# Handing the last 672 columns of the mixer's output weights to nine of the 16 DMA engines

## The chip, the cores and the metric

One core of one Trainium2 chip runs the kernel. The time is the device time of one execution in microseconds, taken as a median of several executions. Differences below 0.3 us matter, so small differences are read from the traces as well as from the times.

## The reference, cut to what matters

A decode step. An attention block (32 query heads, 4 key/value heads, 65,536 cached keys of 128 values) and a small gated mixer work on one row of 1,024 values, and a sigmoid gate mixes their two results.

```python
g = _sigmoid((x * gate_w).sum(-1, keepdims=True))
a = _A_ref(x, A_k_cache, A_v_cache, A_wq, A_wo)     # attention over the caches
b = _B_ref(x, B_w_in, B_w_sp, B_b_sp, B_w_out)      # mixer: B_w_out is 1792 x 1024
return g * a + (1 - g) * b
```

The caches and the weights are 162 MB, each byte read once. For a single row of queries there is little arithmetic, so the work is to stream those bytes (before the change the loads fill 98.9% of the span of 16 DMA engines).

## The kernel before

All large loads go through one queue, in a fixed order, into slots of a ring in SBUF. A load of 128 rows is one instruction on the sync engine (SP):

```python
def load(keys, src, off):
    n = len(stream)
    w = src.shape[1]
    ...
    stream.append((keys, off, src))

load([("wq", 0)], rows(A_wq, 0, 8), VB)
load_k2(0, 0)
load([("win", 0)], rows(B_w_in, 0, 8), VB)
load_k(2, 2)
load_k(3, 0)
load([("wout", 0)], rows(B_w_out, 0, 14), VB)      # 128 rows of 14 x 1024 columns, 28,672 bytes each
...                                                # caches, then the attention's output weights
# in issue():
P("SP", lambda e, o=OFF["RING"] + off, w=w, src=src: e.dma_start(arena[:, o:o + w], src),
  w=[("slot", x) for x in gr], dma="s%d" % gr[0])
```

The last six loads are the attention's output weights. Matmuls on them, one copy and a store of 2 KB end the program.

## Time and profile before

| | before |
|---|---|
| median time, us | 381.85 (381.81 to 382.06, 6 runs) |
| span of the profiled run, us | 380.3 |
| share of 16 DMA engines' span that the loads fill | 98.9% |
| landings of the last load, first and last engine, us | 376.57 and 378.23 |
| mean landing of the last load over 16 engines, us | 377.49 |

A landing is the moment at which one DMA engine reports that its share of a load has arrived, by an increment of the load's semaphore; the last load, of 128 rows, has 16 of them in the trace, as has every other load of 128 rows. PE is the matmul engine, DVE the vector engine. The main lines of the page stand in the prediction below. Two more views of the kernel before matter later. The first is the sync engine's queue in order of time (start us, us, engine and line, operation, out<-in, count): the load that the change cuts is issued at 65.81, and nothing more is issued until 79.62.

```profile
65.81 0.33 SPq L389 DMA_DIRECT2D arena<-in_B_w_out_dram  x1
79.62 0.33 SPq L389 DMA_DIRECT2D arena<-in_A_k_cache_dram  x1
```

The second is the DMA view of 84.5 to 87.3 us, the time in which the last rows of that load run (queue and kind: packets, MB, share of 16 engines):

```profile
q1 hardware_dynamic: 37, 1.19, 100.1%
```

A packet counts in the window in which it starts, with its whole duration, so a share can pass 100%. What is to be read is the ratio of the last two numbers: here 1.19 MB took 100.1% of 16 x 2.8 us, which is 37.7 us of engine time for a MB. This is the price of undisturbed streaming.

### The profile page before, as it was taken

To read this page: it belongs to the slowest core of one execution; us is meant where nothing else is said; L and a number is where in the kernel's file an instruction comes from. 1 tells how busy PE (TensorE), PEld (TensorE's weight loads), DVE (VectorE), ACT (ScalarE), POOL (GpSimd) and SP (SyncE) were. 2 spreads that over 40 slices of the span, in tenths; PEclk is the share of its full clock that TensorE was granted. 3 is DMA by queue.
4 is the path that set the end of the run, shared out by engine and by line. 5 is a ranking of instruction groups with operands and counts; after the bars stand their busy time and mean duration, and the time that the engine had idled before them with its cause. 6 is when DMAs were issued, how large, how long until landed. Compare 5 with 4: busy or idle time off the path is not lost.

```text
span 380.3 us, 2581 instructions
## 1 busy us (share of the span) xinstructions
PE 235.1 (62%) x1449; PEld 58.1 (15%) x836; DVE 204.6 (54%) x162; ACT 23.3 (6%) x24; POOL 8.4 (2%) x37
## 2 busy tenths in 40 slices
PE   0061388458558924895788138952895884739378
PEld 0010011011111200122112001220121110212015
DVE  4011496778389525965892249745774882312020
ACT  1000000010420000002200000022000000220000
POOL 5000000000000000000000000000000000000000
PEclk9998599696859985998699859995899697958689
DMA  9999999999999999999999999999999999999996
GB/s 435 427 420 400 469 388 438 441 469 431 401 414 441 441 443 427 434 410 424 477 441 434 434 434 414 415 441 441 434 407 433 445 441 441 436 403 424 419 426 262
DMA packets 4254, 162.17 MB, mean 426 GB/s; under 512 B 532, under 2 KB 532, under 8 KB 788
## 3 DMA queue, kind: packets, MB, share of 16 engines
q1 hardware_dynamic: 4208, 162.01, 98.9%
q8 instruction: 9, 0.15, 0.2%
q10 hardware_dynamic: 36, 0.00, 0.0%
q14 instruction: 1, 0.01, 0.0%
HBM read 162.01 MB, written 0.00 MB: 426 GB/s over the span
## 4 chain that ended last, share of the span: by engine, by line
DMA 56%; PE 23%; DVE 18%; ACT 1%; issue 1%; SPq 0%; ACTq 0%; DVEq 0%
DMA arena<-in_A_k_cache_dram 34%; DVE arena L502 15%; DMA arena<-in_A_wo_dram 10%; DMA arena<-in_A_v_cache_dram 8%; PE scp L260 7%; PE scp L262 6%; DMA arena<-in_B_b_sp_dram 5%; PE obt L260 4%; PE obt L262 4%; DVE arena L539 1%; PE fbt L712 1%; PE fbt L660 1%; ACT arena L534 1%; SPq L389 0%; ACTq L288 0%
## 5 line engine op out<-in xcount | busy, mean ns | idle before, releaser
L502 DVE STREAM_TRANSPOSE arena<-arena 128x2048 f32<-128x2048 f32 x64 | 143.0, 2284 | 48.2 <-DMA arena<-in_A_k_cache_dram 32.7
L260 PE MATMUL scp<-arena 128*128 128x512 bf16 (+1 forms) x275 | 112.8, 429 | 87.7 <-DVE arena L502 86.3
L262 PE MATMUL scp<-arena 128*128 128x512 bf16 (+1 forms) x279 | 113.1, 427 | 0.0
L260 PE MATMUL obt<-arena 128*64 128x512 bf16 (+2 forms) x334 | 62.9, 419 | 17.5 <-DMA arena<-in_A_v_cache_dram 17.5
L262 PE MATMUL obt<-arena 128*64 128x512 bf16 (+2 forms) x334 | 62.2, 414 | 0.0
L260 PEld LDWEIGHTS scp<-arena 128*128 128x128 bf16 (+1 forms) x275 | 27.7, 104 | 200.1 <-issue 101.3
L539 DVE STREAM_TRANSPOSE arena<-arena 128x2048 bf16<-128x2048 bf16 x7 | 16.2, 2311 | 28.5 <-PE obt L262 26.4
L534 ACT ACTIVATE arena<-arena 128x2048 bf16<-128x2048 f32 x8 | 16.0, 2002 | 218.6 <-DVE arena L531 195.6
L260 PEld LDWEIGHTS obt<-arena 128*64 128x64 bf16 (+1 forms) x334 | 18.3, 113 | 70.7 <-issue 56.1
L519 DVE TENSOR_SCALAR_CACHE_REDUCE arena<-scp 128x2048 f32<-128x2048 f32 x8 | 18.3, 2292 | 16.0 <-PE scp L262 16.0
L580 PE MATMUL mbt<-arena 128*128 128x128 bf16 x16 | 1.9, 258 | 12.6 <-DVE arena L575 12.6
L542 DVE STREAM_TRANSPOSE arena<-arena 128x1024 bf16<-128x1024 bf16 x2 | 2.5, 1246 | 12.7 <-PE obt L262 12.7
L490 POOL COPY arena<-arena 32x32 bf16<-32x32 bf16 x16 | 3.2, 203 | 234.5 <-PE scp L262 209.7
L568 DVE RECIPROCAL arena<-mbt 128x1 f32<-128x1 f32 x4 | 0.6, 139 | 14.1 <-PE mbt L563 14.1
L531 DVE TENSOR_REDUCE arena<-mbt 128x1 f32<-128x32 f32 x4 | 0.8, 192 | 13.5 <-PE mbt L528 13.5
L437 PE MATMUL mbt<-arena 1*128 1x2 bf16 x1 | 0.2, 158 | 12.3 <-DMA arena<-in_B_b_sp_dram 12.3
L439 DVE COPY arena<-mbt 128x2 f32<-128x2 f32 x1 | 0.2, 160 | 12.3 <-PE mbt L437 12.3
L775 DVE CAST arena<-fbt 36x128 bf16<-36x128 f32 x1 | 0.3, 283 | 11.0 <-PE fbt L712 11.0
L432 PE MATMUL scp<-arena 8*128 8x1 bf16 x8 | 0.7, 199 | 8.7 <-DVE arena L427 8.7
L712 PE MATMUL fbt<-arena 128*32 128x128 bf16 x128 | 4.1, 220 | 0.1
L712 PEld LDWEIGHTS fbt<-arena 128*32 128x32 bf16 x128 | 3.6, 97 | 1.6 <-DMA arena<-in_A_wo_dram 0.8
L467 DVE CAST arena<-obt 97x1024 bf16<-97x1024 f32 x1 | 1.2, 1225 | 4.9 <-PE obt L262 4.9
(91 smaller groups left out, 54.2 us busy)
## 6 DMA issues: line engine op xcount, KB each, us to landing
arena<-in_A_k_cache_dram SPq DMA_DIRECT2D x6, 4096.0 KB, 33.1
arena<-in_A_v_cache_dram SPq DMA_DIRECT2D x2, 4096.0 KB, 26.0
arena<-in_B_w_in_dram SPq DMA_DIRECT2D x1, 7168.0 KB, 30.4
arena<-in_A_wo_dram SPq DMA_DIRECT2D x3, 2048.0 KB, 33.4
arena<-in_B_w_out_dram SPq DMA_DIRECT2D x1, 3584.0 KB, 21.5
arena<-in_A_wo_dram SPq DMA_DIRECT2D x1, 1280.0 KB, 30.3
arena<-in_A_wo_dram SPq DMA_DIRECT2D x1, 512.0 KB, 31.0
arena<-in_A_wo_dram SPq DMA_DIRECT2D x1, 256.0 KB, 30.8
```

The source lines that it names most:

```text
L260: return e.matmul(*a, **kw)
L262: one = e.matmul(*a, **kw).ins
L467: P("DVE", lambda e: e.tensor_copy(psb[0:97, :], ob[0:97, :]), w=["psb", "ob"])
L490: P("POOL", lambda e, pb=pb: e.tensor_copy(vw(qpad, 24 + 32 * pb, [[QP, 4], [1, 8]], 32 * pb, 32), vw(qall, 8 * g, [[32, 4], [1, 8]], 32 * ...
L502: P("DVE", lambda e: e.transpose(ktb(i).bitcast(F32), sl[:, 4096 * p:4096 * (p + 1)].bitcast(F32)), r=keys[4 * p:4 * p + 4], w=[("kt", i % ...
L519: P("DVE", lambda e: e.tensor_scalar(scs(j), scp[:, :], 0.0, None, op0=ALU.add, op1=ALU.max, accum_out=maxc[:, j:j + 1]), w=[("sc", j % 2) ...
L534: P("ACT", lambda e: e.activation(psb2, scs(j), ACTF.Exp, bias=gcol(j // 2, K_NB), scale=SCALE, accum_out=lp[:, j:j + 1]), r=[("sc", j % 2 ...
L539: P("DVE", lambda e: e.transpose(ptsb2, psb2), r=["psb"], w=[("ptsb", 0), ("ptsb", 1)])
L542: P("DVE", lambda e: e.transpose(ptsb(n), ab("PSB", 1024, 1024 * (n % 2))), r=["psb"], w=[("ptsb", n % 2)])
L580: ins = e.matmul(mb[:, 0:128], sel[:, 128 * c:128 * (c + 1)], osc[:, 128 * c:128 * (c + 1)], start=(c == 0), stop=(c == 3))
L660: ins = e.matmul(fb[32 * b:32 * (b + 1), 0:QW], e4z[0:97, 31 - j:63 - j], part[0:97, QW * s:QW * (s + 1)], start=(first and s % (NW // 2) ...
L712: ins = e.matmul(fb[32 * b:32 * (b + 1), 0:QW], ovz[:, z:z + 32], sl[:, o:o + QW], start=False, stop=(i == 3 and c == 7), tile_position=(0 ...
```

## The change

Its intent is to even out when the 16 DMA engines finish. The last 672 of the 14,336 columns are cut off and loaded as three further loads of 69, 54 and 5 rows, so that some engines carry more and the others less.

```diff
-    def load(keys, src, off):
+    def load(keys, src, off, cut=None):
...
+        dst = arena[:, OFF["RING"] + off:OFF["RING"] + off + w]
+        parts = [(dst, src)]
+        if cut:
+            c, heights = cut
+            parts = [(dst[:, 0:w - c], src[:, 0:w - c])]
+            p = 0
+            for h in heights:
+                parts.append((dst[p:p + h, w - c:w], src[p:p + h, w - c:w]))
+                p += h
+            assert p == 128
+        stream.append((keys, off, w, parts))
...
-    load([("wout", 0)], rows(B_w_out, 0, 14), VB)
+    load([("wout", 0)], rows(B_w_out, 0, 14), VB, cut=(672, (69, 54, 5)))
...
-            P("SP", lambda e, o=OFF["RING"] + off, w=w, src=src: e.dma_start(arena[:, o:o + w], src),
-              w=[("slot", x) for x in gr], dma="s%d" % gr[0])
+            P("SP", lambda e, todo=todo: [e.dma_start(dst, x) for dst, x in todo],
+              w=[("slot", x) for x in gr], dma="s%d" % gr[0], parts=len(todo))
```

The rest of the diff lets one recorded operation issue several loads and count all their completions on one semaphore.

More of the change, by code (lines that the diff above doesn't have):

```diff
@@ L29, in __init__, with op @@
         self.early = 0
-    def op(self, eng, fn, r=(), w=(), dma=None):
+    def op(self, eng, fn, r=(), w=(), dma=None, parts=1):
         o = Op()
@@ L50, in op @@
         if dma is not None:
-            self.dma_count[dma] = self.dma_count.get(dma, 0) + 16
+            self.dma_count[dma] = self.dma_count.get(dma, 0) + 16 * parts
             o.dma = (dma, self.dma_count[dma])
@@ L112, in run @@
                 if o.dma:
-                    last.then_inc(dsem[o.dma[0]], 16)
+                    for x in last if isinstance(last, list) else [last]:
+                        x.then_inc(dsem[o.dma[0]], 16)
                 elif o.inc:
@@ L312, in load @@
             place[key] = (n, off + i * (w // len(keys)), w // len(keys))
-        stream.append((keys, off, src))
+        dst = arena[:, OFF["RING"] + off:OFF["RING"] + off + w]
[9 more added lines that the diff above has]
+        stream.append((keys, off, w, parts))
     def rows(w, i, c):
@@ L379, in issue @@
             n = issued[0]
-            keys, off, src = stream[n]
-            w = src.shape[1]
+            keys, off, w, todo = stream[n]
             gr = grains(off, w)
```

## The prediction

- The numbers of engines are names. 0 to 7 are the eight chains that carry the first store's packets (eight landings, 376.11 to 377.59 us: four early, one middle, three late). That the three engines of the 69 rows, 0 to 2, lie among these eight was the assumption.
- That 69, 54 and 5 rows run on 3, 9 and 5 engines was not in the trace of before. The trace after the change bears it out: 33 packets of 4 bytes where 16 stood (the 480 of the program before are 16 for each of 29 loads of 128 rows and 8 for each of two stores of 8 rows), which is 16 + 3 + 9 + 5, and short rows on nine chains of 16, so that the loads of 69 and of 5 rows run on engines of the load of 54. The 23 + 6 + 1 = 30 rows on each of three engines are an estimate from these counts.
- "Ports" is the name of the first rival. It says that engines 9 to 15, "those", slow down by what they were spared.

The last engine's end goes from 1.79 to 1.46 us behind the first, 0.33 us, and 381.96 - 0.33 = 381.63 was put at 381.7.

> **What bounds the kernel now.** I read the page first: the DMA row of the 40 slices, the queue table, the chain that ended last. Then the chain in order of time for the last 14 us, and last the trace's records of single DMA packets and of semaphore landings. Three parts of the page:
>
> ```profile
> span 380.3 us, 2581 instructions
> ...
> DMA  9999999999999999999999999999999999999996
> ...
> q1 hardware_dynamic: 4208, 162.01, 98.9%
> q8 instruction: 9, 0.15, 0.2%
> ...
> DMA 56%; PE 23%; DVE 18%; ACT 1%; issue 1%; SPq 0%; ACTq 0%; DVEq 0%
> ```
>
> The reader is to see that the 16 DMA engines never rest: the queue of loads (q1) fills 98.9% of 16 engines' span, and PE (62%) and DVE (54%) have room. 162 MB over 380 us is 426 GB/s, so only bytes, or an uneven share of them, can move the end. Small beside q1 stand nine instruction packets (q8); I use them below. The tail of the chain in order of time (start us, us, what):
>
> ```profile
> 331.05 37.33 DMA arena<-in_A_wo_dram
> 368.38 0.04 issue
> 368.42 0.39 PE scp L260 x4
> ...
> 376.41 0.08 issue
> 376.50 1.77 PE fbt L712 x56
> 378.27 0.01 issue
> 378.27 0.42 PE fbt L712 x8
> 378.69 0.03 issue
> 378.72 0.02 DVEq L110
> 378.74 0.04 issue
> 378.79 0.28 DVE arena L775
> ```
>
> The reader is to see that PE starts at 368.42 on the landing of an output-weight block and has no real pause afterwards; the last 8 matmuls start at 378.27, when the last load has just landed (378.23). So the end follows the last loads one to one. And the DMA share in windows over the last microseconds (window; us, PE, PEld, DVE, ACT, POOL, PEclk, DMA share, GB/s):
>
> ```profile
> 375.00:376.00 1.00, 1.00 (x26) 0.58 (x19) 0.00 (x0) 0.00 (x0) 0.00 (x0) 1.00 0.98 393
> 376.00:377.00 1.00, 0.92 (x21) 0.54 (x21) 0.00 (x0) 0.00 (x0) 0.00 (x0) 1.00 0.65 257
> 377.00:378.00 1.00, 1.00 (x43) 0.97 (x38) 0.00 (x0) 0.00 (x0) 0.00 (x0) 1.00 0.41 150
> ```
>
> The share falls from 0.98 to 0.65 to 0.41 ahead of the last landing: some engines have run out of work while others still carry the last rows. That is the only slack the change can use.
>
> **How uneven it is.** The 16 increments of the last load's semaphore land at 376.57, .57, .60, .61, .65, then 376.96 and 377.07, then nine from 377.89 to 378.23. So five engines end 1.6 us before the last, two 1.2 to 1.3 us, nine within 0.35 us of it. The first load shows a spread of only 0.51 us (21.435 to 21.949). The lateness is collected on the way: each 16 KB instruction packet (at 55.3, 102.3, 133.6, 189.5, 245.2, 287.4, 329.6 and 370.3 us, 1.0 to 1.1 us each; the ninth comes at 377.7) is followed by one landing of the set moving from its place to 1.4 to 1.8 us; an 8 KB packet of another queue at 85.6 us does the same to one more, by 1.0. Eight and one make the nine late ones. As every engine always has rows waiting, a loss is never made up. Balancing at best ends at the mean: (5 x 376.60 + 376.96 + 377.07 + 9 x 378.09) / 16 = 377.49, so 0.74 us, 0.2% of the span, is the ceiling of any such change.
>
> [...]128 rows use 16 engines, 69 use 3, 54 use 9, 5 use 5; the store of 8 rows uses 8. The trace agrees for the cases it has: its 256-byte store packets lie on eight chains of packets. [...]
>
> **Who is late.** [...] Following the packets (each starts 4 ns before the one ahead of it on its engine ends), engines 0 to 7 hold four early ends, one middle one (+0.6 us) and three late (+1.4 to +1.5 us after the first); engines 8 to 15 hold one early, one middle (+0.5) and six late (+1.55 to +1.8). [...] Which numbers the others have the trace does not say. I choose to believe that the split was made to fit: engines 0 to 2 early, and the late ones of the upper half among 9 to 15.
>
> **The change part by part.** Removed: 128 x 1344 bytes from the one output-weight load of the mixer. From packets of 2,048 and 4,096 bytes (starts 80 and 155 ns apart) a byte costs 0.0366 ns and a packet 5 ns, so 1,344 bytes cost 49 ns inside a long row and 54 ns as a row of their own (an estimate).
> - All 16 engines lose 8 x 49 = 0.39 us.
> - Engines 0 to 2 gain 23 + 6 + 1 = 30 rows: 30 x 54 = 1.62, net +1.24 us with the extra semaphore packets.
> - Engines 3 and 4 gain 7 rows, 0.38: net 0. Engines 5 to 8 gain 6, 0.32: net -0.06. Engines 9 to 15 gain nothing: net -0.39.
> - Three more issues on the sync queue at 0.33 us each, 1.0 us, after the one at 65.81. The next issue there comes at 79.62, so they are hidden. The weights land at 85.7 to 87.3 and their matmuls run at 97.7, so a landing 1 us later is hidden too.
>
> At the end, counted from the first engine's end (late ones 1.41 to 1.79): the upper six go from 1.56-1.79 to 1.17-1.40; the lower three from 1.41, 1.48, 1.52 to at best 1.35, 1.42, 1.46; engines 0 to 2 from at most 0.1 to about 1.34. The last is now 1.46 instead of 1.79: the sum is 0.33 us. The landing at 368.38 that starts PE's tail holds the same engines, bar the one not delayed until 370.3, and moves by 0.3, so PE follows. That is 381.96 - 0.33 = 381.63 if the numbers fit.
>
> **Rivals.**
> - [...] those slow down by what they were spared. For it: an engine moves 65,536 bytes in 2,414 ns, 27.1 GB/s, all alike[...]. Against: nothing in this trace. It would make the time 381.9 to 382.1.
> - *A late engine lies among 0 to 2.* Then it gets +1.24 on top of 1.4 to 1.5, and the end moves out by 0.9 to 1.0 us: 382.9. For it: two of the lower half's early chains do take instruction packets late (329.6, 370.3) and their numbers are unknown. Against: [...] the split would make no sense. Were the middle one among 0 to 2, it would end at 1.85, and nothing is won: 382.0.
> - *The rows are slower than estimated*, since they begin in the middle of the block of a row: at 60 ns engines 0 to 2 end at 1.5, and the gain is 0.25.
> - *The transfer is hidden anyway* at its own place (the weights wait 10 us for their use). True, but the queue is full from there to the end, so the shift of each engine lasts.
>
> **Range and chances.** I give the fitting split 0.55 (381.6 to 381.75), ports or a middle engine 0.30 (381.9 to 382.1), a late engine among 0 to 2 0.10 (about 382.9), anything else 0.05. The three runs before spread by 0.25 us. Predicted 381.7, with 381.4 to 382.2 to hold it 8 times in 10. Two per cent is 7.6 us, ten times the ceiling of 0.74 and more than any loss I can name: within 2% at 0.98, 0.01 on either side.
>
> **What would show it.** Right: the last load's landings lie within about 0.5 us for twelve or more engines instead of nine, with the first landing near 376.6 still but only two to four early; three chains with 30 packets of 1,344 bytes; the DMA share in the last full microsecond before the end over 0.5; the last matmuls start 0.3 us sooner. Wrong: packets of engines 9 to 15 that lengthen while the short rows run (ports), 1,344-byte packets over 60 ns, an engine landing 1 us behind all others (a late one among 0 to 2), or instruction packets that fall on other engines than before, which would undo the fit.

## The result, and the profile after

| | before | after |
|---|---|---|
| median time, us | 381.85 | 382.45 (382.21 to 382.67, 6 runs) |
| span of the profiled run, us | 380.3 | 381.1 |
| first and last landing of the last load, us | 376.57, 378.23 | 377.11, 378.96 |
| mean landing of the last load, us | 377.49 | 378.27 |

The kernel became slower by 0.60 us; by the 2% limit it is the same. The ratio is 1.0014 with a 95% interval of 1.0002 to 1.0027. Ratios here are the mean time of one kernel's fast runs over that of the other's of the same rounds, so not quite the ratio of the medians that are quoted. The prediction said 381.7 with 381.4 to 382.2: the sign was wrong and the result lies outside its range.

The page of the changed kernel, the lines that answer to those of before:

```profile
span 381.1 us, 2582 instructions
...
DMA packets 4399, 162.17 MB, mean 426 GB/s; under 512 B 549, under 2 KB 677, under 8 KB 933
...
q1 hardware_dynamic: 4353, 162.01, 98.9%
q8 instruction: 9, 0.15, 0.2%
```

The same 162.01 MB fill the same 98.9% of a span that is 0.8 us longer. So the engines are not idle for longer; the bytes have become dearer. The end of its chain in order of time (start us, us, what):

```profile
345.99 31.09 DMA arena<-in_A_wo_dram
377.08 0.14 issue
377.22 1.78 PE fbt L722 x56
379.00 0.01 issue
379.00 0.42 PE fbt L722 x8
...
379.51 0.28 DVE arena L785
```

The final 8 matmuls start at 379.00 instead of 378.27, again right after the last landing (378.96). The end still follows the loads. The last microseconds in windows, the columns as in the prediction (the last two: DMA share, GB/s):

```profile
376.00:377.00 1.00, 0.59 (x2) 0.01 (x1) 0.00 (x0) 0.00 (x0) 0.00 (x0) 1.00 0.88 353
377.00:378.00 1.00, 0.78 (x29) 0.81 (x31) 0.00 (x0) 0.00 (x0) 0.00 (x0) 1.00 0.73 284
378.00:379.00 1.00, 1.00 (x35) 0.79 (x29) 0.00 (x0) 0.00 (x0) 0.00 (x0) 1.00 0.18 59
```

These windows must not be laid beside those of 375 to 378 us before, as the end has moved by 0.73 us. The DMA view of the two microseconds ahead of the last landing, before (376.23 to 378.23) and after (376.96 to 378.96):

```profile
q1 hardware_dynamic: 144, 0.32, 41.1%
```

```profile
q1 hardware_dynamic: 168, 0.34, 43.5%
```

The engines run dry hardly less than before. Four landings come before 378 us (377.11, .31, .32, .60) and twelve between 378.16 and 378.96; before, there were seven early ones and nine late. So bytes were moved onto early engines, as intended, but the last landing still lies 0.69 us behind the mean, where it lay 0.74 us behind, and the mean itself moved by 0.78 us. The last landing moved by their difference, 0.73 us. The whole loss arises at the cut: the mean landing of the load just ahead of it was 77.43 us before and 77.40 after, that of the load just behind it 105.45 and 106.24.

The window of 84.5 to 87.3 us shows where. After the change:

```profile
q1 hardware_dynamic: 179, 1.28, 136.1%
```

Now 1.28 MB take 136.1% of 16 x 2.8 us, 47.6 us of engine time for a MB, a quarter more than before. The trace's records of single packets add up to nearly the whole loss:

| packets (bytes) | undisturbed, us | after the change, us | lost over all engines, us |
|---|---|---|---|
| 128 short rows (1,344) | 0.058 | 0.075 mean, up to 0.101 | 9.62 - 128 x 0.058 = 2.2 |
| 128 long rows of the same load (27,328) | 1.013 to 1.022 (the first experiment below) | up to 1.34 | 130.8 - 130.0 = 0.8 |
| rows of the next load (65,536) | 2.418 | twelve of 3.04 to 3.34, four of 2.63 to 2.71 | 10.3 - 1.0 (before) = 9.3 |

That is 12.3 us in all, or 0.77 us for each of 16 engines, and the mean landing moved by 0.78 us. (All packets of the queue together took 13.4 us longer than before.) The nine 16 KB instruction packets come at nearly the same times as before (53.4 to 378.5 us), so they are not the difference: between the two loads just named lie one of them (100.6 us, 102.3 before) and an 8 KB packet of another queue (85.5 us, 85.6 before), in both kernels. The question for the experiments is why rows that other engines move slow everybody down.

### The profile page after: what moved, and what is told of

The parts are those of the page before. It is cut to its first block, busy times and chain, and to the rows that moved or that the text cites. A ratio compares the mean times of both kernels' runs of the same rounds, so it can differ in the third digit from the quotient of the medians.

```text
span 381.1 us, 2582 instructions
## 1 busy us (share of the span) xinstructions
PE 232.3 (61%) x1447; PEld 57.7 (15%) x836; DVE 204.3 (54%) x162; ACT 23.2 (6%) x24; POOL 9.4 (2%) x37
## 3 DMA queue, kind: packets, MB, share of 16 engines
q1 hardware_dynamic: 4353, 162.01, 98.9%
HBM read 162.01 MB, written 0.00 MB: 425 GB/s over the span
## 4 chain that ended last, share of the span: by engine, by line
DMA 64%; DVE 18%; PE 17%; issue 1%; ACTq 0%; SPq 0%; DVEq 0%
DMA arena<-in_A_k_cache_dram 41%; DVE arena L512 16%; DMA arena<-in_A_v_cache_dram 10%; DMA arena<-in_A_wo_dram 8%; DMA arena<-in_B_b_sp_dram 5%; PE scp L261 5%; PE scp L263 4%; PE obt L261 3%; PE obt L263 3%; DVE arena L549 1%; PE fbt L722 1%; ACTq L289 0%; DVE arena L583 0%; DVE arena L585 0%; SPq L399 0%
## 5 line engine op out<-in xcount | busy, mean ns | idle before, releaser
L261 PE MATMUL scp<-arena 128*128 128x512 bf16 (+1 forms) x273 | 110.4, 421 | 85.8 <-DVE arena L512 85.3
L263 PE MATMUL scp<-arena 128*128 128x512 bf16 (+1 forms) x279 | 111.0, 416 | 0.3 <-issue 0.3
L541 DVE TENSOR_REDUCE arena<-mbt 128x1 f32<-128x32 f32 x4 | 0.8, 191 | 13.8 <-PE mbt L538 13.8
```

Of the source, the lines that this page charges most:

```text
L261: return e.matmul(*a, **kw)
L263: one = e.matmul(*a, **kw).ins
L541: P("DVE", lambda e: e.tensor_reduce(gcol(g, K_NB), mb[:, 0:32], AXX, ALU.min), w=[("nb", g), "mb"])
```

## The experiments

**The theory (named "ports" in the expectations).** In a full load each engine keeps to places in SBUF of its own. A row handed to another engine is written beside the stream of whoever owns its place, and both wait. That places have owners is an assumption, which no trace shows; the runs can show which arrangements of rows lengthen the packets. **The rivals:** short rows that begin at an odd place cost; more loads on the queue cost; the three engines with the most rows (0 to 2 in the expectations) simply got too many bytes; each handed row has a fixed cost. "Before" in each group is the kernel before, run on the same chip in the same rounds.

### Is it the short rows, the number of loads, or who writes them?

```diff
-cut=(672, (69, 54, 5))
+cut=(672, (128,))       # x1: the 672 columns as one load of all 128 rows
+cut=(672, (64, 64))     # x2: as two loads of 64 rows, 4 rows on each of 16 engines
+cut=(7168, (128,))      # x3: half the tensor, one load of 128 rows
+cut=(7168, (64, 64))    # x4: half the tensor, two loads of 64 rows
```

> The same 672 columns as a second load, but of all 128 rows on 16 engines[...]. Theory ports [...]: no collision, the 65,536-byte packets behind it stay at 2.42 us, short rows at 58 ns, end +0.05 to +0.15 us against the kernel before (about 381.95). Rival short rows (1,344-byte rows that begin in the middle of a block row are what costs): the packets of that microsecond stretch as in the changed kernel, +0.5 us (382.4). Rival more loads on the queue: about +0.2.

> The 672 columns as two loads of 64 rows, each on all 16 engines, 4 rows an engine: every engine moves exactly the bytes of before, but 64 rows reach only half of the partitions. Theory ports: short rows stretch from 58 to about 100 ns and packets of 65,536 bytes beside them lengthen by 0.2 to 0.7 us; end +0.2 to +0.6 us (382.05 to 382.45) though no engine has more bytes. Rival uneven bytes (engines 0 to 2 have become the late ones): as x1, about 381.95. Rival short rows: as the changed kernel, 382.4.

> Half of the tensor, 7,168 columns, as a second load of 128 rows on 16 engines: rows of 14,336 bytes. Both theories: nothing changes, 381.85 to 382.0, packets of 14,336 bytes at about 0.53 us. It is the control for x4.

> The same 7,168 columns as two loads of 64 rows on 16 engines, long rows (14,336 bytes), no engine with more bytes than before. Theory ports: [...] the packets of 14,336 bytes take up to 1.05 us instead of 0.53, and the end moves out by 1 to 4 us (383 to 386). Rival short rows, rival uneven bytes, rival more loads: as x3, 381.9 to 382.0.

| run | median, us | before, us | difference | one row of the 672 or 7,168 columns, us | lengthening of the 65,536-byte rows, sum us |
|---|---|---|---|---|---|
| x1 | 381.92 | 381.82 | +0.10 | 0.058 to 0.059 | 1.2 |
| x2 | 382.35 | 381.82 | +0.53 | 0.068 mean, up to 0.112 | 7.7 |
| x3 | 381.83 | 381.82 | +0.01 | 0.535 to 0.548 | 1.0 |
| x4 | 388.00 | 381.82 | +6.18 | 1.05 mean, up to 1.26 | 13.8 |

The sum in the last column is the time over 2.418 us of all such rows between 80 and 100 us; the kernel before has 1.0 there. x1 has the same short rows in the same place and costs next to nothing, so short rows and a second load are out. In x2 and x4 each load has 16 packets of 4 bytes (48 of them from 82 to 92 us in x2, 32 in x1; in x4 the whole program has 32 more than before). So all 16 engines take part in each, with 4 of 64 rows if they share alike, as they do with 128 rows (8 on each of 16 chains before the change). No engine then moves a byte more than in x1 and x3, and an overload of three engines is not needed for a loss. x4 is the strongest: against x3 one load of 128 rows became two of 64, and it lost 6 us, more than the 1 to 4 us expected. If its rows took twice the 0.535 us of x3, the 8 on each engine would lose 8 x 0.535 = 4.3 us (an estimate). The rows did take about twice as long (1.05 us). With the 65,536-byte rows behind them the packets' own sum is (202.9 - 137.6 + 13.8 - 1.0) / 16 = 4.9 us on each engine, and the mean landing of the last load moved by 5.1 us. The rest of the 6 us is that the engines end more unevenly: the last landing is 1.7 us behind the mean, where it was 0.7.

### Bytes or rows? And does the relief arrive at all?

```diff
-cut=(672, (69, 54, 5))
+cut=(336, (69, 54, 5))      # x5
+cut=(1344, (69, 54, 5))     # x6
+cut=(640, (69, 54, 5))      # x7: the rows begin at a multiple of 256 bytes in memory
+cut=(672, ())               # x8: the columns are not loaded (wrong result on purpose)
```

> The change with rows half as wide (336 columns, 672 bytes), heights 69, 54, 5 as they are. In the changed kernel the 65,536-byte packets beside the short rows took 10.3 us more than 2.418 us each, summed over all engines. Theory port by bytes: that sum halves to about 5 us, and the end is +0.2 to +0.3 us against before (382.1). Rival fixed cost per row handed over: the sum stays at 9 to 10 us, the end +0.5 to +0.7 us, as half of the relief is gone too (382.4).

> The change with rows twice as wide (1,344 columns, 2,688 bytes). Theory port by bytes: the lengthening of the 65,536-byte packets grows to about 20 us in sum and engines 0 to 2, with 30 rows of at least 0.105 us, become the last: end +1 to +1.8 us (383.2). Rival fixed cost per row: the sum stays near 10 us; engines 0 to 2 still carry +2.4 us, end +0.6 to +0.9 us (382.6).

> The change with 640 instead of 672 columns, so that the short rows begin at a multiple of 256 bytes of the memory they are read from (27,392) instead of 27,328. Theory ports: as the changed kernel, a twentieth less: +0.45 to +0.6 us (382.4), short rows at 55 ns undisturbed and 70 to 75 on the mean. Rival odd start of the rows: short rows at 52 ns, their mean near it, end +0.0 to +0.2 us (381.95).

> The last 672 columns are not loaded at all (wrong result on purpose: the matmuls read what the slot held before). It measures the relief by itself: 8 x 1,344 bytes less on every engine. If each engine's saving reaches the end, as the prediction held, -0.39 us (381.45). If the ends are held by something else, 381.8.

| run | handed row, bytes | median, us | before, us | difference | lengthening, less 1.0 of before, sum us |
|---|---|---|---|---|---|
| x5 | 672 | 382.04 | 381.83 | +0.21 | 4.0 |
| the change | 1,344 | 382.45 | 381.85 | +0.60 | 9.3 |
| x6 | 2,688 | 384.28 | 381.83 | +2.45 | 19.8 |
| x7 | 1,280 | 382.24 | 381.83 | +0.41 | 9.4 |
| x8 | none | 381.39 | 381.83 | -0.44 | 0.0 |

The lengthening doubles with each doubling of the bytes, so a fixed cost of a row is out. x6 ends later than its expected 383.2: the mean landing of its last load moved by 1.67 us, and the landings now spread over 3.15 us. By the 95% interval of the ratio x5 (0.9992 to 1.0018) and x8 (0.9976 to 1.0001) are not clear of noise; in their traces the mean landing of the last load moved by +0.34 and -0.47 us. In x7 the short rows still took 0.075 us on the mean, though undisturbed ones took 0.055; where they begin in memory is not the cause. x8 tells that one term of the prediction was right: 8 x 1,344 bytes less on every engine, worked out as 0.39 us, shorten the program by 0.44.

### Which rows, and on which side?

Next, 3,584 columns (rows of 7,168 bytes). x9 and x10 cut rows 0 to 63 into eight loads of 8 rows, both followed by the same load of rows 64 to 127. x11 and x12 write like x9 and x10, but read the other one's rows, with a wrong result. The edits, shortened:

```diff
+x9:  low = [slice(p0 + q, p0 + 32, 4) for p0 in (0, 32) for q in range(4)]   # every fourth row
+x10: low = [slice(8 * q, 8 * q + 8) for q in range(8)]                       # neighbours
+x11: writes as x9, reads as x10        x12: writes as x10, reads as x9
     for x in low + [slice(64, 128)]:
         parts.append((dst[x, w - c:w], src[x, w - c:w]))
```

> The last 3,584 columns (rows of 7,168 bytes) as one load of rows 64 to 127 on 16 engines, the same in all four kernels of this group, and eight loads of 8 rows [...] for rows 0 to 63, each of every fourth row (0, 4, ... 28 and so on)[...]. Theory ports: these 64 rows run undisturbed at about 0.27 us; what is lost is the upper half's collision and its 4 rows on each lower engine, +1 to +2.5 us (383 to 384.3). Rival that loads on fewer engines are slow as such: as x10.

> As x9, but each of the eight loads takes 8 neighbouring rows (0 to 7, 8 to 15, ...)[...]. Same loads, rows, bytes and engines. Theory ports: [...] rows stretch from 0.27 to about 1 us, the end +4 to +7 us against x9 (388 to 391). Rival: same as x9.

> As x9 in what is written (every fourth row), but read from neighbouring rows of the source (wrong result on purpose). If the collision is on the side that writes to SBUF: as x9. If it is on the side that reads: as x10.

> As x10 in what is written (neighbouring rows), but read from every fourth row of the source (wrong result on purpose). If the collision is on the side that writes to SBUF: as x10. If it is on the side that reads: as x9.

| run | median, us | before, us | difference | mean of a 7,168-byte row, us |
|---|---|---|---|---|
| x9 | 386.67 | 381.88 | +4.79 | 0.477 |
| x10 | 387.27 | 381.88 | +5.39 | 0.628 |
| x11 | 386.42 | 381.88 | +4.54 | 0.477 |
| x12 | 387.51 | 381.88 | +5.63 | 0.584 |

This failed as a test of the rows. x9 was built on an assumption about which rows belong to one engine, which no trace shows, and its rows were to run undisturbed at 0.272 us. Only the first did; from 83.9 to 85.2 us the rows took 0.50 to 0.57. Seven 65,536-byte rows beside them took 4.95 to 5.15 us instead of 2.42. Neither x9 nor x10 met its expectation. That the loads of 8 rows run on eight engines is in the trace of x9: 96 packets of 4 bytes from 82 to 92 us, which is 16 + 16 + 8 x 8. What holds is that the order of reading matters little: x11 goes with x9 (+4.54 and +4.79 us), x12 with x10 (+5.63 and +5.39), as they write.

Since loads of 8 rows might be slow for another reason, the next five runs tested that assumption and its rivals (edits shortened again). x17 asks whether x4 lost its 6 us because each of its loads writes one half of the rows.

```diff
+x13: low = [slice(q, 64, 8) for q in range(8)], then rows 64 to 127           # every eighth row
+x14: low = [slice(q, 128, 8) for q in range(8)]                               # 16 rows, every eighth
+x15: low = [slice(16 * q, 16 * q + 16) for q in range(8)]                     # 16 neighbours
+x16: eight loads of all 128 rows, 448 columns each
+x17: 7,168 columns as two loads of 64 rows: slice(0, 128, 2), slice(1, 128, 2)
```

> As x9, but the eight loads for rows 0 to 63 take every eighth row (0, 8, ... 56)[...]. If an engine serves eight neighbouring rows: these rows run at 0.27 us instead of 0.55, and the end comes 1 to 3 us before x9 (383.5 to 385.7). If it serves rows as x9 took it, or if loads on 8 engines are slow as such: as x9 or worse (386.5 or more).

> All 128 rows of the 3,584 columns in eight loads of 16 rows on 16 engines, every eighth row (0, 8, ... 120), no engine with more bytes than before. If an engine serves eight neighbouring rows: no collision, rows at 0.27 us, 381.8 to 382.1 in spite of nine loads. If it serves rows as x9 took it: [...] +2 us or more (384).

> As x14, but each load takes 16 neighbouring rows, written by 16 engines. Same loads, rows, bytes and engines as x14. Ports of eight neighbouring rows: [...] rows 3 to 8 times as long, +4 us or more (386 or more). Rival more loads or short loads: as x14.

> The 3,584 columns of x14 and x15 as eight loads too, but each of all 128 rows and 448 columns (rows of 896 bytes). If the number of loads costs: +4 us as x14 and x15 (386). If it is the arrangement of rows over engines: only the 56 extra packets of 5 ns on each engine, +0.3 to +0.5 us (382.2).

> As x4 (two loads of 64 rows, 7,168 columns, 16 engines), but one load takes the even rows and one the odd rows, so that each reaches partitions of all groups of eight. If x4 lost its 6 us [...]: back at 381.9 to 382.5. If any arrangement other than the full load's costs: about 388 again.

| run | median, us | before, us | difference | mean of a cut row, us (undisturbed) |
|---|---|---|---|---|
| x13 | 386.98 | 381.74 | +5.24 | 0.535 (0.272) |
| x14 | 385.84 | 381.74 | +4.10 | 0.514 (0.272) |
| x15 | 385.92 | 381.74 | +4.18 | 0.563 (0.272) |
| x16 | 382.00 | 381.80 | +0.20 | 0.041 (0.041) |
| x17 | 381.88 | 381.80 | +0.08 | 0.542 (0.535) |

x13 and x14 speak against engines that serve eight neighbouring rows: their rows were to take 0.27 us by that, and took 0.535 and 0.514, about twice as long. x15 ended like x14, with rows twice as long and not three to eight times, so its expectation failed in that, and alone it would have left the number of loads as a rival.

x16 against x14 and x15: nine loads in each, and the same bytes on each engine (144 packets of 4 bytes from 82 to 92 us in x14 and in x16, 16 for each load). With all 128 rows in each load it costs 0.20 us, with 16 rows in each 4.1. So the number of loads is out, and the arrangement of rows is what costs. x17 against x4 is the cleanest pair: two loads of 64 rows on 16 engines in both, even and odd rows for +0.08 us, halves for +6.18. The DMA view of both from 82 to 92 us, first x4, then x17 (packets, MB, share of 16 engines):

```profile
q1 hardware_dynamic: 150, 2.46, 101.1%
```

```profile
q1 hardware_dynamic: 177, 4.52, 105.4%
```

About the same engine time moved 2.46 MB in x4 and 4.52 MB in x17. The same view of x14 and of x16:

```profile
q1 hardware_dynamic: 321, 3.34, 110.0%
```

```profile
q1 hardware_dynamic: 1235, 4.47, 109.5%
```

x16 has four times as many packets and moves a third more.

x4 and x17 differ in the rows they read as well as in those they write. The last run writes as x4 and reads as x17 (wrong result):

```diff
+    for x in (slice(0, 128, 2), slice(1, 128, 2)):
+        y = slice(64 * (x.start % 2), 64 * (x.start % 2) + 64)
+        parts.append((dst[y, w - c:w], src[x, w - c:w]))
```

> Two loads of 64 rows, 7,168 columns, on 16 engines: written to the halves as in x4, read from the even and the odd rows as in x17 (wrong result on purpose). If the collision is where SBUF is written: as x4, about 388, with packets of 14,336 bytes up to 1.26 us. If it is where memory is read: as x17, about 381.9.

It took 387.79 us against 381.89 before, +5.90, with cut rows of 1.08 us on the mean and up to 1.33: like x4 (1.05 and 1.26). In this pair the loss goes with the rows that are written in SBUF, not with those that are read from memory.

**What stays open.** Which rows exclude one another is not settled. The assumption behind x9 did not hold in x9 itself (0.477 us a row where 0.272 was to come), and the rows of x10 lengthened less than was expected from it (0.628 us, not about 1). If an engine had eight neighbouring rows instead, x9 and x17 would be explained, but x13 and x14 would have run undisturbed. So what the rows share that makes them wait is not shown: the runs show which arrangements cost, not why. Which row of a load of 8 or 16 rows goes to which engine is not in the trace. No run gives the change's own loads of 69, 54 and 5 rows another arrangement: that they collide as those of x2 and x4 do is read from their packets and from x5 to x7. No experiment pointed to a version that beats both kernels with a right result: evening out by this means hands rows to other engines, and every run that handed rows over lost more than it won. Giving the engines uneven bytes without handing rows over would need another layout of the weights and was not tried; its ceiling is the 0.74 us of the prediction.

**What the trace does settle: were the three engines with the most rows early?** The trace does not name engines, but in the changed kernel these three can be told: their short rows go on, three at a time, to 86.97, 87.05 and 87.20 us, where all others have ended by 85.65. They start their second row of the next load 1.7 to 1.9 us after the first engine does. By the prediction's reading an instruction packet alone puts an engine 1.4 to 1.8 us behind the first. One of the three that had met such a packet too, earlier or later, would lie about 3 us behind (an estimate from the two). But no landing of any later load lies more than 2.13 us behind the first of its set. So in the profiled run all three were early ones.

## Why the prediction was wrong, point by point

- **What bounds the kernel: right.** The loads fill 98.9% of the engines' span in both kernels, and the last matmuls start on the last landing in both.
- **The ceiling and the unevenness: right as a reading.** Three of the early engines joined the late ones, as planned. The loads also ran on as many engines as worked out: 33 packets of 4 bytes in the window where 16 stood before, which is 16 + 3 + 9 + 5.
- **"All 16 engines lose 8 x 49 = 0.39 us": right.** x8 measured 0.44 us.
- **Hidden issues and an early landing of these weights: right.** The four issues take 1.44 us from 65.74, and the next comes at 79.43. Their matmuls start at 97.16, and no wait on that load stands before them.
- **The cost of a short row, 54 ns: a little low.** Undisturbed it is 58 ns, for 30 rows 0.1 us. In the changed kernel the mean was 75 ns.
- **The step that failed: "Engines 9 to 15 gain nothing: net -0.39" and "Engines 5 to 8 gain 6, 0.32: net -0.06".** The working added up each engine's bytes as though engines did not touch one another. The rows of the next load on the other engines, twelve of them 0.62 to 0.92 us longer, took back more than the 0.39 us. On the mean each engine lost 0.77 us. Nor were the ends evened out: of the 0.33 us that this was to win, the last landing came 0.05 us closer to the mean (0.69 us behind it instead of 0.74).
- **The rival whose sign came true, with its size wrong.** The one named "ports" was given 381.9 to 382.1, since the engines spared the rows would "slow down by what they were spared". Twelve rows of the next load lengthened by about twice that: 0.62 to 0.92 us where 0.39 was spared. In all 12.3 us were lost, where the bytes cut off are worth 128 x 49 ns = 6.3 us of engine time. With twice the size this rival would have said about 382.35 (an estimate: the prediction's 381.96 and 0.39 us more). The sign to look for was named beforehand, packets of other engines that lengthen while the short rows run, and that is what the trace shows. That ports are the reason is not shown.
- **Short rows that are slow as such, and a late engine among 0 to 2:** the first is refuted by x1 and x7. The second is ruled out by the landings, as said above; nor is its sign there, an engine landing 1 us behind all others (the last two land at 378.88 and 378.96).

## What to carry to other kernels

With the DMA engines 98.9% busy, moving bytes from late engines to early ones was not free here: a row handed to another engine is still written at the old place, and beside a full stream it cost about twice its bytes (12.3 us of engine time lost, for bytes worth an estimated 6.3). Before cutting a load into fewer rows than 128, try the cut into even and odd rows, or into columns, beside the one into blocks of neighbouring rows: the first two cost 0.0 to 0.2 us here (x1, x3, x16, x17) and the last up to 6 us (6.18 in x4). A wide spread alone is not enough, as every eighth row cost 4.1 us (x14). When the ceiling of a change is 0.2% of the time, look for what it may disturb before adding up what it saves.
